# Soft-capped attention and a mixture of attention experts on one core: a bank for each warm-up product, batch 6's exponentials in loose halves, second-stage scores first, new due offsets

## The chip, the cores and the metric

The kernel runs on one NeuronCore of a Trainium2 chip. Its time is the device time of one execution in microseconds (us); before the change the median of 3 runs is 305.93 us (305.67 to 306.42).

## The reference

There are two stages. The first is attention with a soft cap, over 8 batches, 12 heads, 448 positions and 64 values a head:

```python
scores = scale * np.matmul(q, k.transpose(0, 1, 3, 2))
scores = cap * np.tanh(scores / cap)            # cap = 30
attn = np.exp(scores - scores.max(-1)); attn /= attn.sum(-1) + 1e-9
x = heads_side_by_side(np.matmul(attn, v))      # [8, 448, 768]
```

The second is a mixture of 4 attention experts, of which each position uses the best 2. Each expert is one causal head of 64:

```python
logits = x @ w_gate                             # top 2 of 4, softmax over the two: w
q, k, v = x @ wq[e], x @ wk[e], x @ wv[e]
a = causal_softmax(scale * q @ k.T)
out += w[e] * (a @ v @ wo[e])                   # only where e is among the two
```

The whole output is 8 x 448 x 768 in float32. Tiles in the kernel are float16, sums are float32.

## The kernel before, in words

**First stage.** The 12 heads of a batch are 6 pairs; over 8 batches these are pairs 0 to 47, called `p`. For each pair the queries and keys are loaded, cast, and transposed; TensorE forms the transposed scores (keys on the partitions, L956 to L972) in PSUM tiles X and Y, of three banks each (two for Y in the last part); ScalarE takes tanh from X or Y into the tile `yp` (L1018), and then exp of all of the pair in place (L1030). No maximum is subtracted, as the cap bounds the scores. TensorE multiplies with the values and a column of ones (L1044, L1051, L1091, L1098), VectorE divides (`rca`, `xk`), and the result is transposed to `xT` by TensorE or by a DMA. From pair 2 to pair 39 two pairs go together. In batch 7 the pairs 42 to 47 take only 320 of the 448 queries, and two further units 48 and 49 take the last 128 queries of all six pairs.

**Second stage.** When a batch's six pairs are done, its values, gate logits (L1196), keys and queries (L1204) come from `xT`. The gate is worked out on POOL, and becomes masks `mB` that blank the queries of experts not chosen; the masks are transposed (`mT`), and multiplied with the queries (`qm`). `b_score` (L1394) forms the scores of one half (`s` = 0 or 1, the first or the second choice) in 18 products over two banks (`H1` and `H0`, L1386), and one exp of 1024 columns writes them into `pB` (L1415). POOL blanks what is not causal, `b_pv` multiplies with the values (L1465), VectorE divides and weighs (`oB`, L1480), `b_ot` adds the halves (`oS`) and transposes them (`oT`), and `b_wo` multiplies with `wo` (L1527), copies to `ob` and stores. In units of pairs, batch 6's two halves stand at 46 and 48. Batch 7 is done apart, in `last` and `last2` (L1614, L1769), with its own exps into `pB` (L1691) and `p2` (L1815), its own `oB`-like sums in `normed` (L1552) and its last stores at L1602 and L1608.

**What sets the order.** The program builds a graph of all operations and a planner (`Graph.solve`) lays them out once, one list for each engine. ScalarE's tanh and exp are a fixed chain (`fixed=True`): their order is given, and their times in the plan give all other operations a due time, backwards along the graph. Of the operations that could start at once, an engine takes the one whose due time is earliest. `RANKS` adds offsets in hundredths of a us to the due times of single operations, by their number in the graph, from a given time of the plan on. An operation marked `first` (L1987) may be taken ahead of another one that was chosen, if its due time is near. PSUM has eight banks: A0 and A1, the third A2 (which is closed until `third` at pair 39 and then comes from Y), and those of X and Y. A `Group` holds a bank from its first operation to its last; `AUX` allows the A banks, `ANY` those of X and Y too, when their tile is not in use. On each engine instructions run in the order of the list, and an instruction that waits holds up what is behind it.

**Warm-up.** Products of a tile of zeros (`warm`) keep TensorE busy at the start: 6 of 512 columns and 35 of 128 (L1853), which have no due time but for the six:

```python
    gw = Group(AUX)
    for i in range(NWARM + NFILL):
        n = 512 if i < NWARM else 128
        pe(n, lambda n=n: nc.tensor.matmul(
            bank(gw)[:, 0:n], warm[:, 0:128], warm[:, 0:n], start=True, stop=True), ["warm"],
```

Of the kernel before, what the change touches and what calls it, by code (L numbers as in the profile page):

```python
# [25 lines left out]
    (7.5, {  # L26
        65: 646, 108: 767, 186: -94,
    }),
    (21.5, {
        191: -129, 322: 14,  # L30
    }),
    (35.5, {
        357: 88, 368: 348, 466: 221, 468: -411,
    }),
    (63.5, {
        432: 516, 554: 343, 616: 258,
    }),
    (77.5, {
        636: 695, 646: -603, 703: -641, 709: -990, 791: -13,
    }),  # L40
    (91.5, {
        810: 50, 820: 125, 873: -73, 877: -38, 880: -476,
    }),
    (105.5, {
        695: -612, 697: 532, 820: -377, 822: 211, 912: -369, 929: 381, 933: 464, 939: 1598, 949:
        515, 1026: -513, 1029: 895, 1036: 150, 1055: -784,
    }),
    (119.5, {
        976: 122, 983: 380, 990: 288, 1096: 302, 1097: 304, 1108: -37, 1109: -244, 1111: 407,
        1117: 1079, 1196: 125, 1200: 248,  # L50
    }),
    (133.5, {
        990: -504, 1009: -179, 1018: 602, 1145: -627, 1204: 594, 1205: 864, 1235: 444, 1262:
        966, 1378: -79,
    }),
    (147.5, {
        1018: -435, 1355: -175, 1359: -105, 1397: 756, 1421: -173, 1425: 295, 1431: -335, 1433:
        -92, 1437: 872, 1441: 173, 1443: 362,
    }),
    (161.5, {  # L60
        1330: 578, 1331: 361, 1344: 359, 1519: -107, 1805: -241, 1807: 149,
    }),
    (175.5, {
        1451: -385, 1456: -1234, 1463: 792, 1466: 578, 1468: 493, 1469: 793, 1579: 170, 1585:
        188, 1589: -354, 1594: 120, 1671: -161, 1674: -217, 1676: 517, 1680: 202, 1722: -164,
        1723: 589,
    }),
    (189.5, {
        1753: 139, 1760: 416, 1762: 562, 1837: 67, 1839: 107, 1843: 115,
    }),  # L70
    (203.5, {
        1777: 61, 1780: -527, 1782: -302, 1785: -404, 1839: -41, 1842: 96, 1843: -53, 1908: 233,
        1990: 117, 1993: 67, 1997: 19,
    }),
    (217.5, {
        2061: -122,
    }),
    (231.5, {
        2158: 275,
    }),  # L80
    (214.5, {
        1962: 381, 1993: 51, 1997: 83, 2086: -336, 2118: 159, 2137: -314, 2150: 1017, 2164: 31,
        2203: -393,
    }),
    (234.5, {
        2086: -835, 2161: 510, 2175: 657, 2178: 474, 2321: 577, 2324: -805, 2325: 1282, 2348:
        254, 2433: 776,
    }),
    (254.5, {
        2509: 2924, 2534: 784, 2546: 1060, 2592: -43, 2607: -322, 2609: 1259, 2615: 497, 2618:  # L90
        766, 2621: 193, 2649: 665, 2697: 184, 2707: 616, 2708: 1147, 2719: 640, 2738: 163,
    }),
# [4 lines left out]
    }),  # L97
    (239.5, {
        2155: 215, 2262: 380, 2315: 184, 2467: -521, 2499: 159, 2524: 1446, 2525: 657, 2564:
        -320, 2583: 594, 2592: 251, 2599: 529, 2600: -250, 2607: 619, 2620: 146, 2644: 1040,  # L100
        2653: 535, 2707: 430, 2738: 432,
# [4 lines left out]
SAIL = 1.1  # L106
SHIP = 1.25
# [4 lines left out]
NWARM = 6  # L112
# [15 lines left out]
XDUE = (4.354, 8.0)  # L128
# [265 lines left out]
def kernel(  # L394
# [44 lines left out]
    def sb(name, shape, dt=f16):  # L439
        return pool.tile(shape, dt, name=name)  # L440
# [100 lines left out]
    def turned(n, dst, src, r, w, name, due=None):  # L541
# [55 lines left out]
        "p (e c t) -> p e c t", e=E, c=4)  # L597
    oTL = [sb(f"oTL{i}", [128, 2, 128]) for i in range(3)]
# [412 lines left out]
    alone = {0, 1, *exps}  # L1011
# [343 lines left out]
    def b_mask(b, s):  # L1355
# [9 lines left out]
        if b < MD:  # L1365
            for r in range(2):
# [8 lines left out]
                pe(0, mm, [("mB", s), "ident"], [("mt", b, s, r)], g, occ=0.22, name=f"mT{b}")  # L1375
# [18 lines left out]
    def b_score(b, s):  # L1394
        x = b % 2
        z = "X" if b >= LB - 2 else flip()
        for part, bk in ((H1, z + "1"), (H0, z + "0")):
            for i, (o, c, q0, n) in enumerate(part):
                def mm(o=o, c=c, q0=q0, n=n):
                    ps = whole(z)[:, o // 512, :]  # L1400
# [9 lines left out]
                lead = i == 0 and part is H1  # L1410
                pe(0, mm, [("kB", x, r) for r in range(2)] + [("qm", qi(x, s), r) for r in range(2)]
                   + ([] if lead else [("z", z)]), [("s", bk)] + ([("z", z)] if lead else []), occ=2 * c_pe(n), name=f"sB{b}_{s}", takes=ZB[z] if lead else ())
        pi = 2 * (b % 2) + s
        pb = pB[pi]
        act(c_act(1024), lambda: nc.scalar.activation(  # L1415
            pb[:, 64:], TILE[z][:, 0:2, :].rearrange("p a c -> p (a c)"), AF.Exp, scale=isc),
            [("s", z + "0"), ("s", z + "1")], [("pB", pi)], fixed=True, name=f"eB{b}_{s}",
            frees=ZB[z])
        b_score.last = fixed_last()
# [35 lines left out]
    def b_pv(b, s):  # L1455
        x = b % 2
        pi = 2 * (b % 2) + s
        for n in range(4):
            g = Brief(ANY, 1.6)
            cs = cols(n)  # L1460
            for i in range(0, len(cs), 2):
                def mm(g=g, i=i, cs=cs):
                    for t in range(i, min(i + 2, len(cs))):
# [3 lines left out]
                            vB[x][:, c, :, :], start=(t == 0), stop=(t == len(cs) - 1),  # L1467
                        )

                pe(0, mm, [("pB", pi), ("pB", pi, 0), ("pB", pi, 1), (b, f"mw{s}")] + [("vB", x, c) for c, _ in cs],  # L1470
                   [("pvB", b, s, n)], g,
                   occ=0.11 * len(cs[i : i + 2]), name=f"pvB{b}_{s}")
            k_ = (2 * s + n) % 4
# [559 lines left out]
```

## Time and profile before

| what | value |
|---|---|
| median of 3 runs | 305.93 us (305.67 to 306.42) |
| profiled execution, own time | 304.88 us |
| its span, first to last instruction | 303.1 us |
| ScalarE busy | 288.8 us (95%) |
| TensorE busy | 281.1 us (93%) |
| VectorE busy | 212.4 us (70%) |
| POOL busy | 189.5 us (63%) |
| data moved by DMA | 53.12 MB, mean 175 GB/s |

The profile is one execution. Its times run from the first instruction. PE is TensorE's products, PEld its weight loads, DVE is VectorE, ACT is ScalarE, POOL is GpSimd, SP is SyncE. A row of the list of waits reads: engine, tile and line that waited, who released it, and then us in total, times, and the longest. A row of the instructions in order of time reads: start in us, duration in us, engine, line, operation, what it writes and reads, and in brackets the time that the engine stood still before it and what ended that. Rows that hold several instructions (x2 and more) give the stretch that they cover. A row of the table by stretches reads: the stretch, its length, busy time and number of instructions of PE, PEld, DVE, ACT and POOL, the granted TensorE clock, the busy share of the DMA engines, and GB/s.

### The profile page before, as it was taken

What the parts mean: (1) busy time and instruction counts of PE and PEld (TensorE: products, weight loads), DVE (VectorE), ACT (ScalarE), POOL (GpSimd) and SP (SyncE); (2) the same over time, 40 slices, a digit from 0 to 9 for tenths busy, and PEclk for the clock granted to TensorE, in tenths of its full rate; (3) what the DMA queues carried; (4) which work ended last, traced back from release to release, by engine and by line L of the source; (5) the groups of instructions that cost most, each with busy time, mean ns of one, the idle gap of its engine ahead of it and who ended that gap; (6) DMA issues with size and microseconds to landing.
All of it is one profiled execution on the core that took longest, in us unless ns stands there. A gap on an engine that the chain in (4) does not pass through costs nothing.

```text
span 303.1 us, 8923 instructions
## 1 busy us (share of the span) xinstructions
PE 281.1 (93%) x3464; PEld 191.8 (63%) x3464; DVE 212.4 (70%) x628; ACT 288.8 (95%) x208; POOL 189.5 (63%) x535
## 2 busy tenths in 40 slices
PE   8696979899999999999999999998999999999993
PEld 4353636557765668666776767656675766666761
DVE  2354527557766689588778688588777997687973
ACT  4999999999999999999999999999999999998991
POOL 6883523589955985894679952784479503831490
PEclk9999788999999999999999999999999999999999
DMA  6899989999989288786989666073407382534446
GB/s 174 213 240 195 238 202 271 223 241 260 257 229 229 63 264 224 171 212 141 297 212 193 174 180 226 23 193 118 132 7 106 81 230 33 100 61 160 73 158 208
DMA packets 86874, 53.12 MB, mean 175 GB/s; under 512 B 47536, under 2 KB 83120, under 8 KB 86832
## 3 DMA queue, kind: packets, MB, share of 16 engines
q1 hardware_dynamic: 86448, 52.13, 69.0%
q8 instruction: 27, 0.44, 0.6%
q10 hardware_dynamic: 384, 0.43, 0.4%
q14 instruction: 15, 0.12, 0.2%
HBM read 36.19 MB, written 11.01 MB: 156 GB/s over the span
## 4 chain that ended last, share of the span: by engine, by line
ACT 47%; PE 38%; DVE 9%; issue 2%; DMA 2%; SPq 0%; DVEq 0%; ACTq 0%
ACT yp L1018 23%; ACT yp L1030 22%; PE A L1051 4%; PE Y L963 3%; PE A L1527 3%; PE X L963 3%; PE A L1196 3%; PE A L1204 3%; PE A L1044 2%; ACT pP L1415 2%; DMA qf<-in_q_dram 2%; PE X L972 1%; DVE oB L1480 1%; DVE ob L530 1%; PE X L1405 1%
## 5 line engine op out<-in xcount | busy, mean ns | idle before, releaser
L1030 ACT ACTIVATE yp<-yp 128x6272 f16<-128x6272 f16 (+5 forms) x32 | 133.9, 4187 | 0.0
L1018 ACT ACTIVATE yp<-Y 128x1344 f16<-128x1344 f32 (+3 forms) x70 | 79.9, 1141 | 2.5 <-PE Y L963 2.4
L1018 ACT ACTIVATE yp<-X 128x1344 f16<-128x1344 f32 (+3 forms) x61 | 76.5, 1254 | 0.8 <-PE X L963 0.2
L1051 PE MATMUL A<-v,yp 128*128 128x65 f16 x936 | 48.3, 196 | 0.0
L1051 PEld LDWEIGHTS <-yp 128*128 128x128 f16 x1008 | 45.4, 99 | 3.0 <-issue 1.2
L1044 PE MATMUL A<-vtz,yp 128*128 128x130 f16 x156 | 35.3, 226 | 4.8 <-ACT yp L1030 3.7
L835 POOL CAST v<-vf 128x384 f16<-128x384 f32 x48 | 24.1, 509 | 23.1 <-PE A L1051 12.8
L1073 DVE RECIPROCAL rca<-A 128x4 f32<-128x4 f32 x78 | 14.2, 182 | 34.1 <-PE A L1051 33.7
L1076 DVE TENSOR_TENSOR xk<-A,rca 128x256 f16<-128x256 f32 x78 | 33.0, 424 | 2.4
L799 POOL CAST q<-qf 112x512 f16<-112x512 f32 x44 | 26.7, 618 | 11.5 <-PE A L849 9.0
L1044 PEld LDWEIGHTS <-yp 128*128 128x128 f16 x168 | 16.5, 98 | 20.1 <-issue 13.6
L784 POOL CAST k<-kf 128x384 f16<-128x384 f32 x33 | 16.9, 521 | 15.9 <-DMA kf<-in_k_dram 8.7
L908 DVE COPY qk<-A 128x960 f16<-128x960 f16 x32 | 20.6, 651 | 8.8 <-PE A L849 8.5
L1425 POOL TENSOR_SCALAR_AFFINE_SELECT pP<-pP 128x384 f16<-128x384 f16 x14 | 7.4, 527 | 22.1 <-ACT pP L1415 22.1
L963 PE MATMUL X<-qk 64*128 64x448 f16 x102 | 18.6, 358 | 2.0 <-ACT yp L1018 1.3
L963 PE MATMUL Y<-qk 64*128 64x448 f16 x102 | 19.2, 367 | 1.4 <-ACT yp L1030 0.5
L849 PE MATMUL A<-ident,q 112*128 112x112 f16 x192 | 19.4, 214 | 0.1
L1490 POOL TENSOR_TENSOR oS<-oB,oB 128x512 f16<-128x512 f16 x14 | 16.1, 1154 | 4.4 <-issue 3.8
L1196 PEld LDWEIGHTS <-xT 128*128 128x128 f16 x168 | 15.7, 97 | 3.9 <-issue 1.2
L963 PEld LDWEIGHTS <-qk 64*128 64x128 f16 x204 | 10.3, 93 | 11.4 <-issue 3.7
L1196 PE MATMUL A<-wvg,xT 128*128 128x260 f16 x126 | 17.4, 274 | 0.1
L530 DVE COPY ob<-A 128x384 f32<-128x384 f32 (+1 forms) x30 | 16.2, 552 | 1.8 <-PE A L1527 1.3
(319 smaller groups left out, 677.5 us busy)
## 6 DMA issues: line engine op xcount, KB each, us to landing
qf<-in_q_dram SPq DMA_DIRECT2D x23, 448.0 KB, 6.4
kf<-in_k_dram SPq DMA_DIRECT2D x23, 384.0 KB, 5.2
vf<-in_v_dram SPq DMA_DIRECT2D x23, 384.0 KB, 5.4
out_dram<-ob SPq DMA_DIRECT2D x21, 384.0 KB, 3.2
ktf<-in_k_dram SPq DMA_DIRECT2D x46, 32.0 KB, 4.9
vtf<-in_v_dram SPq DMA_DIRECT2D x46, 32.0 KB, 4.5
out_dram<-ob SPq DMA_DIRECT2D x6, 192.0 KB, 3.2
ob<-in_moe_wv_dram SPq DMA_DIRECT2D x2, 384.0 KB, 5.3
```

The costliest lines, as they stand in the source:

```text
L530: (nc.scalar.copy if o.eng == "ACT" else nc.vector.tensor_copy)(dst(), src())
L799: e(q16[i], qf[s][:, h].rearrange("p h (c d) -> p c h d", c=QC))
L835: nc.gpsimd.tensor_copy(v16[u][:, :, :, 0:Dh], vf[s][:, h].rearrange("p h (c d) -> p h c d", c=KC))
L849: nc.tensor.transpose(ps[:, 0:S].rearrange("m (g c t) -> m c g t", c=QC, t=16)[:, c], q16[i][:, c, :, :].rearrange("p h d -> p (h d)"), id ...
L908: lambda: nc.vector.tensor_copy(qk[t], bank16(g)[:, 0 : S + 512]),
L963: nc.tensor.matmul(dst[:, bank0 + g - gs[0], 0:n], keysT(p)[r, 128 * (c + 1) : 128 * (c + 2)], qk[p % NQK][r, 0:n], start=True, stop=True)
L1018: ACTS[what, p] = act(c_act(n * k), lambda: nc.scalar.activation(y[:, lo : lo + k, 0:n], TILE[z][:, 0:k, 0:n], AF.Tanh, scale=isc / capf), ...
L1030: act(c_act(n * (b - a), False), lambda a=h + a, b=h + b: nc.scalar.activation(y[:, a:b, 0:n], y[:, a:b, 0:n], AF.Exp, scale=capf), ks, ks ...
L1044: nc.tensor.matmul(ps[:, n, :, :], y[:, o : o + 128], vtz[u], start=(n == 0), stop=False, skip_group_check=True,)
L1051: nc.tensor.matmul(ps[:, n, h, :], y[:, o : o + 128], v16[u][:, h, c, :], start=False, stop=(c == 2), skip_group_check=True,)
L1076: dve(c_dve(128 * m), lambda g=g, i=i, rc=rc, m=m: nc.vector.tensor_tensor(xk[p % NXK][:, 2 * i : 2 * i + m, :, :], view(g)[:, 0:m, :, 0:D ...
L1196: nc.tensor.matmul(bank(g)[:, 0 : E * Dh + E], xT[x][:, j, WIN[n] : WIN[n] + 128], wvg[:, j, :], start=(j == j1), stop=(j == jn),)
```

## The change

- The warm-up products: the six of 512 columns share one bank, which is free again behind the sixth, and each of the 35 small ones takes a bank for itself alone.
- Batch 6's two halves (`LOOSE`): the scores of each go to two single banks of any kind in place of tile X, and each bank has its own exp of 512 columns, which is no part of ScalarE's fixed chain. Units 46 and 48 are no longer kept apart from their neighbours (`alone`), so that their products are filled in one go with the next unit's.
- Batch 7's exps write to `pL`, in the upper half of one tanh tile that is free by then, and no longer to `pB`; its weighted sums go to `oBL`, in the tile of the first mask, and no longer to `oB`. So neither waits for batch 6. An empty operation (`pLfree`) stands behind the last reader of that half.
- The score products of the second stage (`sB`) are marked `first`.
- Two orders are added in the graph: the masks' transposes wait for the batch's queries `qB` (and come before their use in `qm`), and a value product waits for the last reader of the reciprocal that its group will write.
- `XDUE` of the second entry goes from 8.0 to 9.5: the due time of the `xT` transposes of units of two pairs.
- `RANKS` is another table: 17 times with 179 offsets, where there were 21 with 178.

```diff
 RANKS = (
-    (7.5, {
-        65: 646, 108: 767, 186: -94,
+    (-0.5, {
+        57: 299, 58: 555, 65: 250, 102: 331, 110: 231, 133: 142, 140: 456, 174: -71, 185: -241,
+        187: -135, 188: -70, 191: -135,
     }),
...
+LOOSE = (0, 1)
...
-XDUE = (4.354, 8.0)
+XDUE = (4.354, 9.5)
...
+    PF = ("yp", (PB + 5) // 2 % 2)
+    free3 = yf[PF[1]][:, 7 * S : 7 * S + 4 * 704].rearrange("p (i c) -> p i c", c=704)
+    pL = [free3[:, 2 * i : 2 * i + 2] for i in range(2)]
+    oBL = mB[0].rearrange("p a b c d -> p (a b c d)").rearrange("p (n e d) -> p n e d", n=4, e=E)
...
-    alone = {0, 1, *exps}
+    alone = {0, 1, *(p for p, (b, s) in exps.items() if b < LB - 1 or s not in LOOSE)}
...
-                pe(0, mm, [("mB", s), "ident"], [("mt", b, s, r)], g, occ=0.22, name=f"mT{b}")
+                pe(0, mm, [("mB", s), "ident", ("qB", x, r)], [("mt", b, s, r), ("qm", qi(x, s), r)], g,
+                   occ=0.22, name=f"mT{b}")
...
+        pi = 2 * (b % 2) + s
+        pb = pB[pi]
+        free = b == LB - 1 and s in LOOSE
         z = "X" if b >= LB - 2 else flip()
-        for part, bk in ((H1, z + "1"), (H0, z + "0")):
+        for part, h in ((H1, 1), (H0, 0)):
+            g = Group(ANY, 1.5) if free else None
             for i, (o, c, q0, n) in enumerate(part):
-                def mm(o=o, c=c, q0=q0, n=n):
-                    ps = whole(z)[:, o // 512, :]
+                def mm(o=o, c=c, q0=q0, n=n, g=g):
+                    ps = bank(g) if g else whole(z)[:, o // 512, :]
...
+            if free:
+                act(c_act(512), lambda g=g, h=h: nc.scalar.activation(
+                    pb[:, 64 + 512 * h : 576 + 512 * h], bank(g), AF.Exp, scale=isc),
+                    [("sf", b, s, h)], [("pB", pi)], g, name=f"eF{b}_{s}")
+        if not free:
+            act(c_act(1024), lambda: nc.scalar.activation(
+                pb[:, 64:], TILE[z][:, 0:2, :].rearrange("p a c -> p (a c)"), AF.Exp, scale=isc),
+                [("s", z + "0"), ("s", z + "1")], [("pB", pi)], fixed=True, name=f"eB{b}_{s}",
+                frees=ZB[z])
...
-                   [("pvB", b, s, n)], g,
+                pe(0, mm, [("pB", pi), (b, f"mw{s}")] + [("vB", x, c) for c, _ in cs],
+                   [("pvB", b, s, n)] + [("rcb", (2 * s + n) % 4)] * (i == 0), g,
...
-            oB[0][:, n], view(g)[:, :, 0:Dh], sl.broadcast_to((128, E, Dh)), ALU.mult),
-            [key, ("slL", n)], [("oB", 0, n)], g, name="oBL")
+            oBL[:, n], view(g)[:, :, 0:Dh], sl.broadcast_to((128, E, Dh)), ALU.mult),
+            [key, ("slL", n)], [("oBL", n), ("mB", 0)], g, name="oBL")
...
-                    pB[pi][:, o : o + W1], bank(g2[e])[:, 0:W1], AF.Exp, scale=isc),
-                    [k0 if e == 0 else ("sL", r, part, 2)],
-                    [("pB", pi, part)] + ([("pB", pi)] if part == 0 else []), g2[e],
+                    pL[r][:, e, o : o + W1], bank(g2[e])[:, 0:W1], AF.Exp, scale=isc),
+                    ["pLfree", k0 if e == 0 else ("sL", r, part, 2)],
+                    [("pL", pi, part)], g2[e],
...
+        pe(0, lambda: None, [], ["pLfree"] + [PF + (7 + w,) for w in range(7)], occ=0.0,
+           name="op")
...
-    gw = Group(AUX)
+    gw = None
     for i in range(NWARM + NFILL):
         n = 512 if i < NWARM else 128
-        pe(n, lambda n=n: nc.tensor.matmul(
+        gw = gw if 0 < i < NWARM else Group(AUX)
+        pe(n, lambda n=n, gw=gw: nc.tensor.matmul(
...
-        o.first = o.name[:2] in ("sX", "sY", "sT", "tr", "qk", "k1", "q1", "ge", "kt")
+        o.first = o.name[:2] in ("sX", "sY", "sT", "sB", "tr", "qk", "k1", "q1", "ge", "kt")
```

More of the change, by code (lines that the diff above doesn't have):

```diff
@@ L47 @@
+    (39.5, {
+        353: 7, 363: 458,
+    }),
+    (55.5, {
+        363: 202, 397: 312, 423: 134, 517: -1175, 554: -388, 573: -91,
+    }),
+    (71.5, {
+        616: 16, 646: -377, 706: 26, 760: 369, 840: 414,
+    }),
+    (87.5, {
+        787: 218, 788: 44, 810: -103, 882: 769,
+    }),
+    (103.5, {
+        695: 942, 943: 646, 1029: 190, 1074: 913,
     }),
     (119.5, {
-        976: 122, 983: 380, 990: 288, 1096: 302, 1097: 304, 1108: -37, 1109: -244, 1111: 407,
-        1117: 1079, 1196: 125, 1200: 248,
-    }),
@@ L102 @@
+    (244.5, {
+        2315: 136, 2499: 43, 2502: -20, 2503: 624, 2517: 165, 2520: -72, 2523: 373, 2527: -330,
+        2528: 303, 2537: 294, 2606: 983, 2622: -414, 2643: -132, 2650: -2605, 2689: -794, 2713:
+        -1257, 2732: -1268, 2745: 1153,
     }),
@@ L1408, in mm @@
                                 )
-                lead = i == 0 and part is H1
+                lead = i == 0 and h == 1 and not free
                 pe(0, mm, [("kB", x, r) for r in range(2)] + [("qm", qi(x, s), r) for r in range(2)]
[L1412 to L1419, printed above, removed]
+                   + ([] if lead or free else [("z", z)]),
+                   [("sf", b, s, h)] if free else [("s", f"{z}{h}")] + ([("z", z)] if lead else []), g,
+                   occ=2 * c_pe(n), name=f"sB{b}_{s}", takes=ZB[z] if lead else ())
+            if free:
[7 more added lines that the diff above has]
+                frees=ZB[z])
         causal(pb, pi, "")
@@ L1572, in mt @@
                     bank16(gt)[:, 128 * r : 128 * (r + 1)],
-                    oB[0][:, n, 2 * r : 2 * r + 2, :].rearrange("p e d -> p (e d)"), ident)
-        pe(0, mt, [("oB", 0, n), "ident"], [("otL", n)], gt, occ=0.11, name="oTL")
+                    oBL[:, n, 2 * r : 2 * r + 2, :].rearrange("p e d -> p (e d)"), ident)
+        pe(0, mt, [("oBL", n), "ident"], [("otL", n)], gt, occ=0.11, name="oTL")
         lo = 64 if n == 2 else 0
@@ L1701, in below @@
                         pattern=[[0, 2], [1, 128]], channel_multiplier=-1)
-                gp(0.38, below, [], [("pB", pi, part) for pi in (2 * r, 2 * r + 1)], name="diagL")
+                gp(0.38, below, [], [("pL", pi, part) for pi in (2 * r, 2 * r + 1)], name="diagL")
+        pe(0, lambda: None, [], ["pLfree"] + [PF + (7 + w,) for w in range(7)], occ=0.0,
+           name="op")
         for part in range(2):
```

73 lines of the change are left out of this document (21 added, 52 removed), and 11 rows, old and new, of the table RANKS.

## The prediction

> **What bounds the kernel now.** I read the page first (busy times, slices), then ScalarE's list of waits, then its instructions in order of time at the head and at the end, then TensorE's and VectorE's beside them, and the table by stretches.
>
> ```profile
> span 303.1 us, 8923 instructions
> PE 281.1 (93%) x3464; PEld 191.8 (63%) x3464; DVE 212.4 (70%) x628; ACT 288.8 (95%) x208; POOL 189.5 (63%) x535
>
> ACT yp L1018 <- PE Y L963: 2.4, 2, 1.8
> ACT pP L1415 <- PE X L1405: 1.7, 2, 1.1
> ```
>
> ScalarE (ACT) is busy for 288.8 of 303.1 us, so 14.3 us is all that it stands still, and only two kinds of waits inside its row of tanh and exp are worth anything: score products that come late (2.4 us, of which 1.8 is the head), and the second stage's scores that come late (1.7 us in two places). The rest is the head before the first tanh and the tail behind the last exp. The table by stretches (PE, PEld, DVE, ACT, POOL busy) says how the end differs from the middle:
>
> ```profile
> 20.00:60.00 40.00, 33.57 (x369) 20.52 (x366) 21.17 (x64) 39.13 (x24) 18.10 (x45) 0.91 1.04 232
> 275.00:280.00 5.00, 4.97 (x73) 3.36 (x72) 3.87 (x9) 3.88 (x4) 0.76 (x2) 1.00 0.21 59
> 280.00:285.00 5.00, 5.00 (x65) 3.92 (x62) 4.65 (x18) 5.00 (x5) 1.34 (x2) 1.00 0.29 84
> 285.00:290.00 5.00, 5.00 (x72) 3.82 (x71) 3.70 (x12) 4.41 (x11) 4.36 (x14) 1.00 0.42 56
> 295.00:303.10 8.10, 2.96 (x24) 1.41 (x22) 3.24 (x10) 1.78 (x5) 0.52 (x2) 1.00 0.61 205
> ```
>
> From 275 to 290 us TensorE has no gap at all, and ScalarE loses 1.12 us at 275 to 280. Behind 295 us nobody is full: that is the latency of the last tile's chain. So ScalarE's row sets when the last exp ends, and the last tile's chain, with TensorE full at its start, adds its length to that.
>
> ```profile
> 274.09 2.11 ACT L1030 ACTIVATE yp<-yp 128x2240 f16<-128x2240 f16 x1
> 277.29 1.02 ACT L1415 ACTIVATE pP<-X 128x1024 f16<-128x1024 f32 x1 [1.08 <-PE X L1405]
> 278.21 0.80 ACT L1018 ACTIVATE yp<-Y 128x768 f16<-128x768 f32 x1
> 283.79 2.54 ACT L1030 ACTIVATE yp<-yp 128x1920 f16<-128x1920 f16 x2
> 293.58 0.63 ACT L1815 ACTIVATE yp<-X0s 128x512 f16<-128x512 f32 x1
> 294.06 0.64 ACT L1815 ACTIVATE yp<-X2s 128x512 f16<-128x512 f32 x1
> 298.96 0.34 SPq L1602 DMA_DIRECT2D out_dram<-kf  x1
> ```
>
> The fixed row ends at 283.79 + 2.54 = 286.33 us; the last store is issued at 298.96, and the span ends 16.77 us behind the last exp. The profiled execution took 304.88 us, 1.78 more than its span; the median of the runs is 305.93, 1.05 above it. I sum against 304.88 and add 1.05 at the end.
>
> **Part 1: the head (a bank for each warm-up product).** Before, all 41 warm-up products share one PSUM bank, which is held until the last of them; as A2 is shut at the start, A1 alone is left for the first transposes.
>
> ```profile
> 4.32 0.41 ACT L818 CAST q<-qf 112x256 f16<-112x256 f32 x1 [0.32 <-DMA qf<-in_q_dram]
> 4.63 0.47 ACT L866 COPY qk<-A 128x384 f16<-128x384 f16 x1
> 5.16 0.53 PE L849 MATMUL A<-ident,q 112*128 112x112 f16 x4
> 6.39 0.22 PE L914 MATMUL A<-ident,ktz 128*128 128x128 f16 x1
> 6.94 0.55 DVE L799 CAST q<-qf 112x512 f16<-112x512 f32 x1 [0.74 <-DMA qf<-in_q_dram]
> 7.41 0.21 DVE L917 COPY qk<-A 128x128 f16<-128x128 f16 x1
> 6.95 0.92 ACT L1018 ACTIVATE yp<-Y 128x896 f16<-128x896 f32 x1 [1.84 <-PE Y L963]
> 8.07 1.29 ACT L1018 ACTIVATE yp<-X 128x1344 f16<-128x1344 f32 x1 [0.20 <-PE X L972]
> 15.15 0.36 PE L963 MATMUL Y<-qk 64*128 64x448 f16 x2 [0.50 <-ACT yp L1030]
> 15.80 0.93 ACT L1018 ACTIVATE yp<-Y 128x896 f16<-128x896 f32 x1
> ```
>
> The q halves are cast by 4.73, but the q transposes (L849) start at 5.16, just behind the copy (4.63 + 0.47 = 5.10) that empties A1. With a second bank they could start at about 4.80: the first tanh moves from 6.95 to 6.59. The second tanh gains only if the tail copy L917 no longer stands behind the cast L799, which waits for its load: the transpose L914 is done at 6.61, a copy then, the tail product (0.36, as the one at 15.15) and the tanh give about 7.4 in place of 8.07. That is the upper bound, 0.67 us. The lower is none: pair 2's first products come at 15.15, ready at 15.51, only 0.29 before ScalarE takes them at 15.80, and a head that is earlier by more has to find them earlier too. I take the middle, -0.35. What is late next is that product.
>
> **Part 2: the second stage's scores first.** Now the planner may put other products between them:
>
> ```profile
> 188.30 0.45 PE L1405 MATMUL X<-qm,kB 128*128 128x256 f16 x4
> 188.59 1.50 PE L1196 MATMUL A<-wvg,xT 128*128 128x260 f16 x12
> 190.81 1.02 ACT L1415 ACTIVATE pP<-X 128x1024 f16<-128x1024 f32 x1 [0.59 <-PE X L1405]
> 33.17 1.29 ACT L1018 ACTIVATE yp<-Y 128x1344 f16<-128x1344 f32 x1 [0.52 <-PE Y L963]
> ```
>
> Twelve value products (1.50) stand between the first four and the other score products, and ScalarE waits 0.59. Marked as first, the scores are chosen ahead of work that is due later. I take -0.5; the ends are -0.59 and +0.5 (a wait like the one at 33.17, if the scores push the first stage's products back). The twelve products are late next, behind them the gate's steps on POOL, for which ScalarE does not wait.
>
> **Part 3: batch 6's exponentials as four loose halves.** Two fixed instructions leave the row. Each keeps ScalarE for 278.21 - 277.29 = 0.92 us, and the second makes it wait for 1.08: -2.92 for the end of the row. Four halves of 512 come in, each worth 294.06 - 293.58 = 0.48. In the row they cost 1.92 and the net is -1.0; behind the row, where ScalarE idles, the net is -2.92. Their due time comes from stores that are due late, so they give way to fixed work, but they will fill a gap where there is one. Between the ends I put two inside and two behind: -2.92 + 0.96 = -1.96. Splitting by itself costs 2 x 0.48 - 0.92 = 0.04 each.
>
> The Trainium skill speaks against the split here ("ScalarE: Activation LUTs", section "What ACT_TABLE_LOAD costs"): an instruction costs 186 ns beside 0.833 ns an element, and back-to-back ones overlap by about 93 ns. By that, an estimate, two halves cost 0.09 us more than the whole, 0.19 for the batch where the rows give 0.08; the sum would be 0.1 us higher. The trace does not bear out so large a price.
>
> **Part 4: the end.** The halves' products go to single banks of any kind in place of tile X, which was held for scores and exp; X's next tanh can be filled earlier. Against this, batch 6's tail work moves back to where TensorE is full.
>
> ```profile
> 265.25 1.06 PE L1405 MATMUL X<-qm,kB 128*128 128x256 f16 x18
> 279.95 0.76 PE L1465 MATMUL A<-vB,pP 128*128 128x260 f16 x5
> 280.55 0.50 PE L1465 MATMUL X0s<-vB,pP 128*128 128x260 f16 x3
> 281.54 0.40 PE L1465 MATMUL A<-vB,pP 128*128 128x260 f16 x2
> 287.08 0.44 ACT L1691 ACTIVATE pP<-X2s 128x320 f16<-128x320 f32 x1
> 105.62 0.63 DVE qB L1191
> ```
>
> One head half's scores are 18 products (1.06), its value products here 0.76 + 0.50 + 0.40 = 1.66. Moved behind 286 they push the last tile's chain by up to 1.66; but as many products of the last batch then move ahead, and from 295 on TensorE works 2.96 of 8.1 us, so much of it fits there. The bounds are -0.5 (X free earlier) and +1.7; I take +0.5. The new buffers (pL in the unused upper half of a tanh buffer, oBL in the mask's tile) let the last batch's exps start before batch 6 is read; now they start at 287.08, over 5 us behind batch 6's value products at 281.54, so nothing is gained by this alone: it only pays for part 3.
>
> Priced at nothing: mask transposes wait for qB (0.63 us on VectorE, four batches; ScalarE never waits there; if one came to the path, 0.63), value products wait for the reciprocal's reader four groups back, XDUE 9.5 delays xT copies by up to 1.5 us, which the batch's end needs much later. The new table of offsets re-orders everything; the one before has 178 offsets, this one 179, so I give it no term, only width.
>
> Sum: -0.35 - 0.5 - 1.96 + 0.5 = -2.31; 304.88 - 2.31 = 302.57; with 1.05, **303.6 us**. Its own range, with half of each term's width, is 302.2 to 305.0.
>
> **The rivals.**
>
> *Banks (slower).* Between 262 and 286 us only three A banks serve transposes, value products and output products. A half holds one from its first product until its exp is done; if ScalarE is in a 2.11 us exp (the row at 274.09), the bank is out for that much longer, and TensorE, in order and without gaps, may stand at a product that has no bank. Behind it stand the next scores, for which ScalarE waits. One half so caught costs up to 2.1 us; two give 303.6 + 4.2 = 307.8. It decides from 3.3 us lost (306.9) on. For it: TensorE 4.97 to 5.00 of 5. Against: tile X, two banks long, is freed.
>
> *The tail eats it (same).* If the last tile's chain, not ScalarE's row, is what TensorE delays, the 1.96 is given back: 305.6. For it: no TensorE gap from 275 to 290 us; against: the 1.12 us that ScalarE stood still there.
>
> *All of it (faster).* Four halves behind the row, the head's bound, no price at the end: 304.88 - 0.67 - 0.59 - 2.92 + 1.05 = 301.8.
>
> *The clock.* The granted clock is 0.91 between 20 and 60 us, and a product takes longer there; ScalarE's 0.52 at 33.17 lies in such a spell (slice digit 7). A third spell gives 303.6 + 0.5 = 304.1, more if it meets several fills. The Trainium skill says why it may move ("TensorE: Matmul & The Clock Gate", section "What's actually happening"): the array runs at half clock until it was busy for a free-running window of some 3.4 us, so changed warm-up products can shift it. The low digits 7, 8, 8 fit that; where the next would fall no row here shows.
>
> **How the numbers follow.** Chances: forecast 0.42, all of it 0.13, the clock 0.07 (these three are faster), the tail 0.13, banks 0.25. No change is told from one by about 0.3% (0.92 us), so faster means below 305.0, slower above 306.9: 0.62, 0.13, 0.25. The range goes to 301.2 below (some 0.04 left out) and to 307.8 above (half of the banks' case left out).
>
> **What would show it.** Part 1: first tanh before 6.7 us, the second before 7.8, and pair 2's first tanh before 15.6. Part 2: no wait of ScalarE behind L1405's products between 100 and 260 us. Part 3: no 1024-wide exp behind 262 us, four of 512 in their place, and the last fixed exp's end at 283 to 285 us. Part 4: from that end to the end of the span 16.5 to 17.5 us. Wrong it would be if ScalarE shows new waits for L956 or L963 behind 262 us (banks), if the tail behind the last exp grows by 2 us or more, or if the new order loses time in the middle, where I left it alone.

## The result, and the profile after

The changed kernel takes 303.13 us (median; 302.53 to 303.42), the one before 305.80 us (305.16 to 306.42) beside it: a ratio of 0.991 with the interval 0.9884 to 0.9936. That is 0.9% faster, and 0.5 us from the forecast of 303.6. The profiled execution took 303.0 us and its span is 301.2, so 1.9 us less than before by both.

The page and ScalarE's list of waits of the kernel after:

```profile
span 301.2 us, 8936 instructions
PE 282.4 (94%) x3464; PEld 191.4 (64%) x3464; DVE 212.5 (71%) x628; ACT 288.5 (96%) x210; POOL 189.8 (63%) x535
```

```profile
ACT yp L1011 <- PE Y L956: 2.0, 2, 1.5
...
ACT yp L1011 <- PE X L965: 0.6, 2, 0.4
```

L1011 is the tanh, L956 and L965 the first stage's score products, L1403 those of the second stage, L1418 the whole exps, L1414 the new halves. ScalarE is as busy as before (288.5 for 288.8); what went is standing still. No wait for `pP` is left.

To see where, I follow the same ScalarE instruction through both traces and subtract its starts. ScalarE's instructions in order of time, after:

```profile
6.61 0.92 ACT L1011 ACTIVATE yp<-Y 128x896 f16<-128x896 f32 x1 [1.49 <-PE Y L956]
7.46 1.29 ACT L1011 ACTIVATE yp<-X 128x1344 f16<-128x1344 f32 x1
10.10 1.29 ACT L1011 ACTIVATE yp<-X 128x1344 f16<-128x1344 f32 x1 [0.43 <-PE X L965]
15.59 0.93 ACT L1011 ACTIVATE yp<-Y 128x896 f16<-128x896 f32 x1
25.09 0.92 ACT L1011 ACTIVATE yp<-X 128x896 f16<-128x896 f32 x1 [0.52 <-PE A L1044]
46.71 1.00 ACT L1011 ACTIVATE yp<-X 128x896 f16<-128x896 f32 x1
184.15 5.74 ACT L1023 ACTIVATE yp<-yp 128x6272 f16<-128x6272 f16 x1
189.47 1.33 ACT L1418 ACTIVATE pP<-X 128x1024 f16<-128x1024 f32 x1
265.68 0.79 ACT L1011 ACTIVATE yp<-Y 128x640 f16<-128x640 f32 x1
271.94 1.23 ACT L1414 ACTIVATE pP<-A 128x512 f16<-128x512 f32 x2
272.93 2.20 ACT L1023 ACTIVATE yp<-yp 128x2240 f16<-128x2240 f16 x1
277.28 1.24 ACT L1414 ACTIVATE pP<-A 128x512 f16<-128x512 f32 x2
278.24 2.62 ACT L1023 ACTIVATE yp<-yp 128x2688 f16<-128x2688 f16 x1
281.26 2.72 ACT L1023 ACTIVATE yp<-yp 128x1920 f16<-128x1920 f16 x2
```

And the rows of the kernel before that answer to them and are not shown yet:

```profile
46.89 0.92 ACT L1018 ACTIVATE yp<-X 128x896 f16<-128x896 f32 x1 [0.25 <-PE X L963]
266.63 1.11 ACT L1415 ACTIVATE pP<-X 128x1024 f16<-128x1024 f32 x1
267.81 0.70 ACT L1018 ACTIVATE yp<-Y 128x640 f16<-128x640 f32 x1
```

| place | before | after | lead | change of it |
|---|---|---|---|---|
| first tanh | 6.95 | 6.61 | -0.34 | -0.34 |
| pair 2's first tanh | 15.80 | 15.59 | -0.21 | +0.13 |
| last tanh of the next two pairs | 23.99 | 25.09 | +1.10 | +1.31 |
| last tanh of the pairs two steps on | 46.89 | 46.71 | -0.18 | -1.28 |
| the exp ahead of one of the second stage's | 184.52 | 184.15 | -0.37 | -0.19 |
| that second-stage exp | 190.81 | 189.47 | -1.34 | -0.97 |
| start of batch 6's last part | 266.63 | 265.68 | -0.95 | +0.39 |
| end of the row, 281.26 + 2.72 | 286.33 | 283.98 | -2.35 | -1.40 |
| end of the span | 303.1 | 301.2 | -1.9 | +0.45 |

So the gain comes from two places, a second-stage exp that no longer waits and batch 6's exps; the head's gain is small, and a loss of 1.31 us at 16 to 25 us is paid back by 47 us. The table by stretches, after (columns as before), shows the end and the place of that loss:

```profile
16.40:19.80 3.40, 1.67 (x16) 1.05 (x16) 0.66 (x1) 3.40 (x3) 3.29 (x18) 1.00 0.96 229
19.80:23.20 3.40, 2.74 (x19) 1.19 (x19) 0.74 (x2) 2.97 (x3) 2.21 (x10) 0.50 1.03 247
23.20:26.60 3.40, 3.40 (x48) 2.93 (x48) 1.59 (x6) 2.80 (x3) 2.20 (x6) 0.50 0.69 149
275.00:280.00 5.00, 5.00 (x76) 4.00 (x74) 4.21 (x15) 5.00 (x7) 0.76 (x2) 1.00 0.00 0
280.00:285.00 5.00, 4.90 (x73) 3.92 (x72) 4.78 (x19) 4.57 (x6) 3.05 (x5) 1.00 0.14 30
```

At 275 to 280 us ScalarE is now busy for 5.00 of 5 us (3.88 before). From 19.8 to 26.6 us the granted clock is 0.50 and ScalarE loses 1.03 us (0.43 and 0.60). Before had two such spells, each half as long, later on:

```profile
30.30:33.70 3.40, 3.36 (x44) 2.54 (x45) 1.57 (x5) 2.88 (x3) 1.57 (x4) 0.53 0.97 232
43.70:47.10 3.40, 3.40 (x40) 2.10 (x38) 1.64 (x6) 3.15 (x4) 0.44 (x2) 0.51 0.95 339
```

The waits at 33.17 and 46.89 lie in them, and after has neither.

### The profile page after: what moved, and what is told of

It is laid out like the page before. It is cut to its first block, busy times and chain, and to the rows that moved or that the text cites. A ratio compares the mean times of both kernels' runs of the same rounds, so it can differ in the third digit from the quotient of the medians.

```text
span 301.2 us, 8936 instructions
## 1 busy us (share of the span) xinstructions
PE 282.4 (94%) x3464; PEld 191.4 (64%) x3464; DVE 212.5 (71%) x628; ACT 288.5 (96%) x210; POOL 189.8 (63%) x535
## 4 chain that ended last, share of the span: by engine, by line
ACT 65%; PE 23%; POOL 4%; issue 3%; DVE 2%; DMA 1%; ACTq 0%; POOLq 0%; DVEq 0%
ACT yp L1023 31%; ACT yp L1011 31%; ACT pP L1418 3%; PE A L1044 2%; PE A L1529 2%; PE Y L956 2%; PE X L956 2%; DMA ktf<-in_k_dram 1%; PE A L1189 1%; PE A L1037 1%; PE A L1871 1%; PE X L1403 1%; PE A L842 1%; PE X L965 1%; PE A L1595 1%
## 5 line engine op out<-in xcount | busy, mean ns | idle before, releaser
L1023 ACT ACTIVATE yp<-yp 128x6272 f16<-128x6272 f16 (+5 forms) x32 | 136.3, 4269 | 0.0
L1011 ACT ACTIVATE yp<-Y 128x1344 f16<-128x1344 f32 (+3 forms) x70 | 85.1, 1216 | 2.0 <-PE Y L956 2.0
L1011 ACT ACTIVATE yp<-X 128x1344 f16<-128x1344 f32 (+3 forms) x61 | 81.6, 1339 | 1.1 <-PE X L965 0.6
L1044 PE MATMUL A<-v,yp 128*128 128x65 f16 x924 | 46.6, 195 | 0.0
L1069 DVE TENSOR_TENSOR xk<-A,rca 128x256 f16<-128x256 f32 x77 | 32.3, 422 | 2.1
L1037 PEld LDWEIGHTS <-yp 128*128 128x128 f16 x168 | 16.5, 98 | 16.0 <-issue 12.9
L956 PE MATMUL X<-qk 64*128 64x448 f16 x102 | 19.4, 371 | 4.2 <-ACT yp L1011 3.4
L519 DVE COPY ob<-A 128x384 f32<-128x384 f32 (+1 forms) x37 | 19.8, 553 | 2.2 <-PE A L1529 1.6
L956 PE MATMUL Y<-qk 64*128 64x448 f16 x102 | 19.2, 368 | 2.1 <-ACT yp L1011 0.8
L956 PEld LDWEIGHTS <-qk 64*128 64x128 f16 x204 | 11.1, 94 | 14.5 <-issue 7.8
L842 PEld LDWEIGHTS <-q 112*128 112x128 f16 x192 | 14.1, 100 | 5.9 <-issue 1.8
L1529 PE MATMUL A<-wo,oT 128*128 128x384 f16 x78 | 17.8, 326 | 0.1
```

Of the source, the lines that this page charges most:

```text
L519: (nc.scalar.copy if o.eng == "ACT" else nc.vector.tensor_copy)(dst(), src())
L842: nc.tensor.transpose(ps[:, 0:S].rearrange("m (g c t) -> m c g t", c=QC, t=16)[:, c], q16[i][:, c, :, :].rearrange("p h d -> p (h d)"), id ...
L956: nc.tensor.matmul(dst[:, bank0 + g - gs[0], 0:n], keysT(p)[r, 128 * (c + 1) : 128 * (c + 2)], qk[p % NQK][r, 0:n], start=True, stop=True)
L1011: ACTS[what, p] = act(c_act(n * k), lambda: nc.scalar.activation(y[:, lo : lo + k, 0:n], TILE[z][:, 0:k, 0:n], AF.Tanh, scale=isc / capf), ...
L1023: act(c_act(n * (b - a), False), lambda a=h + a, b=h + b: nc.scalar.activation(y[:, a:b, 0:n], y[:, a:b, 0:n], AF.Exp, scale=capf), ks, ks ...
L1037: nc.tensor.matmul(ps[:, n, :, :], y[:, o : o + 128], vtz[u], start=(n == 0), stop=False, skip_group_check=True,)
```

## The experiments

The theory is the prediction's: each edit is worth its own term, and the new offsets are only width. The first rival is that an offset table is fitted to one set of rules, so that the parts cannot be told apart under it; others are named where they are tested. Ratios are to the kernel before on the same chip. Where operations are added or left out, the offsets were kept with their operations and not with their numbers.

**One bank for the warm-up products again.**

```diff
-        gw = gw if 0 < i < NWARM else Group(AUX)
+        gw = gw or Group(AUX)
```

> The changed kernel with all 41 warm-up products in one bank again, as before; all else, the offsets too, as changed. Theory A (the gain is made in four places by the four edits, and the head's 0.2 us is the only thing that the banks give): the first tanh goes back from 6.61 to about 6.95 us, the keep-warm products of 512 columns (first at 31.4 in the changed kernel, at 11.8 before) come early again, the half-clock spell of 20 to 27 us goes or shrinks, and with it ScalarE's two waits of 0.52; in sum between 0.2 slower and 1.0 us faster than the changed kernel's 303.1. Theory B (the order from the offsets makes the gain, whatever the edit): the plan no longer fits its offsets and the time is 303.5 to 304.5 with new waits all over.

Measured: 320.72 us, ratio 1.0517 (1.0476 to 1.0557). That is far above what either theory expected. The head shows the mechanism, in a row of TensorE and one of ScalarE:

```profile
5.69 0.36 PE L842 MATMUL A<-ident,q 112*128 112x112 f16 x4 [0.76 <-ACT qk L859]
```

```profile
4.86 0.40 ACT L811 CAST q<-qf 112x256 f16<-112x256 f32 x1 [0.92 <-DMA qf<-in_q_dram]
```

The q transposes wait for the copy that empties the bank, as the prediction had it, and the first tanh starts at 7.16 us, for 6.61 after. Not all of that is the bank's: the load of the queries landed later in this profile, so that their cast starts at 4.86 us and not at 4.32 as in after. And most of the 5% is elsewhere: the planner's order differs from about 4 us on, the later offsets meet another state, and waits appear up to the last batch (one of 5.0 us at L1819). What an edit is worth cannot be read from this kernel.

**The keep-warm products not chained to the warm-up.** After, the 36 large keep-warm products of the middle stand behind the small ones, which wait for banks until 31 us; before they ran from 11.8 us. Is that the cause of the half-clock spell?

```diff
-                   ["warm", ("tick", p, what)], ["warmps"], g, name="fill")
+                   ["warm", ("tick", p, what)], ["keepps"], g, name="fill")
```

> The changed kernel with one key altered: the keep-warm products of 512 columns are no longer ordered behind the 35 small warm-up products. Theory A: the half-clock spell at 20 to 27 us in the changed kernel comes from keep-warm products that are held back behind the small ones, each of which now waits for a bank; freed, they run from about 11 us, the spell goes or is halved, the two waits of 0.52 at 23.3 and 25.1 us shrink, and the time is 302.0 to 302.8. Rival: the spell comes from TensorE's work itself at 17 to 20 us, the keep-warm products find no bank or no gap, and the time stays at 303.1 within 0.4.

Measured: 303.37 us, 0.9942 (0.9918 to 0.9966), the same as after within the intervals. The spell is there all the same; stretch and TensorE row of this kernel:

```profile
20.40:26.80 6.40, 6.34 (x69) 4.31 (x69) 2.52 (x8) 5.36 (x6) 3.06 (x10) 0.50 0.93 178
```

```profile
20.46 0.90 PE L956 MATMUL X<-qk 64*128 64x448 f16 x3 [2.35 <-ACT yp L1011]
```

The keep-warm products now begin at 11.1 us, and TensorE still stands at 18 to 20.46 us with a score product that has no tile. That theory fell. The transposes of the following pairs are half done at that time; that they hold both A banks, so that nothing else can run, is argued and was not tried.

**Batch 6's exps whole and in the chain again, all else as after.**

```diff
-LOOSE = (0, 1)
+LOOSE = ()
```

> The changed kernel with batch 6's two exps whole, fixed and in tile X again (LOOSE empty); offsets kept, each for the same operation. Theory A: ScalarE's row gets back 2 x 0.92 in place of about 1.95 and a wait of up to 1.1 at each of the two; the last fixed exp ends 1.0 to 1.6 us later than 283.98, the stretch behind it stays near 17, and the time is 304.0 to 304.8. Theory B: 303.1 within 0.4.

Measured: 311.22 us, 1.0196 (1.016 to 1.0231). The row of ScalarE that tells it:

```profile
274.06 1.02 ACT L1423 ACTIVATE pP<-X 128x1024 f16<-128x1024 f32 x1 [8.81 <-PE X L1407]
```

Up to 256 us the order on TensorE is that of after. Then one wait of 8.81 us is all of the loss (2.86% more than after, 8.7 us), more than either theory had. The exp's fixed place is at 265 us, but under the new offsets batch 6's queries come at 269.19 (12 products, 2.45 us) and its scores at 272.89 (L1407). After can do that, because a loose exp comes when its scores do (271.94). So the offsets have used the freedom, and the edit and the offsets cannot be priced apart here.

**Second-stage scores not first, all else as after.**

```diff
-        o.first = o.name[:2] in ("sX", "sY", "sT", "sB", "tr", "qk", "k1", "q1", "ge", "kt")
+        o.first = o.name[:2] in ("sX", "sY", "sT", "tr", "qk", "k1", "q1", "ge", "kt")
```

> The changed kernel with the second stage's scores not marked first; offsets kept. Theory A: ScalarE's wait for batch scores in front of the 1024-wide exp near 190 us comes back (0.6 us, 0.97 with what stood before it), and the time is 303.7 to 304.2. Rival: the new offsets already put the scores early, and it is 303.1 within 0.4.

Measured: 311.19 us, 1.0213 (1.0178 to 1.0248). TensorE's order is the same up to about 70 us; from there on ScalarE waits for the scores in one batch after the other:

```profile
ACT pP L1418 <- PE Y L1403: 3.8, 3, 1.6
ACT pP L1418 <- PE X L1403: 2.3, 2, 2.0
```

6.1 us of waits where after has none. At the predicted place the list names POOL:

```profile
193.54 1.02 ACT L1418 ACTIVATE pP<-X 128x1024 f16<-128x1024 f32 x1 [1.01 <-POOL g_h L1304]
```

But its scores (L1403, 18 products from 192.39 us, 1.06 long) end at 193.45, just ahead of it, so this wait may be theirs too. The kind of wait and the place are the predicted ones; the time is not (303.7 to 304.2 was expected), and the size is again edit and misfit together.

**The floor without offsets.** Undoing one edit under a table that was made for it measures the misfit too. So both kernels were run with no offsets, and each with the other's table.

```diff
+RANKS = ()
```

> The kernel before with an empty table of offsets. It is the floor from which the next run is read. The offsets are worth much: the four runs above, where an edit was undone and the offsets kept, were up to 16 us slower, so 312 to 330 us is expected.

> The changed kernel with an empty table of offsets. Theory A (the edits themselves make the gain): 2 to 8 us less than the kernel before without offsets, most of it from the scores that are marked first (waits for the batch scores fewer by 3 us or more). Theory B (only the new table makes it): within 1 us of the kernel before without offsets, or slower.

> The code before with the new offsets, each for the same operation. Theory A, in which edits and offsets were fitted to one another: well over 306, near 311 or more, with waits for the batch scores as where the scores are not marked first, and about 9 us before batch 6's first exp. Theory B: 303 to 304.5.

> The changed code with the offsets of before, each for the same operation. If the edits gain by themselves: 303 to 305. If edits and offsets only fit together: 308 to 322, with a new order from the first microseconds on.

| ratio to before (interval) | no offsets | table of before | table of after |
|---|---|---|---|
| code before | 1.0494 (1.0459 to 1.0528) | 1 | 1.054 (1.05 to 1.0579) |
| code after | 1.0333 (1.0301 to 1.0365) | 1.0384 (1.0343 to 1.0426) | 0.991 (0.9884 to 0.9936) |

One per cent is 3.06 us here. Without offsets the edits give 1.0494 - 1.0333 = 1.6%, or 4.9 us. Each table gives its own code a lot (4.9%, 15.1 us, before; 1.0333 - 0.991 = 4.2%, 12.9 us, after) and the other code nothing (1.054 and 1.0384, neither below its floor). So "the offsets re-order everything" holds, but they are no mere width around the edits: counted along the column without offsets, the 0.9% of the change are 1.6% from the edits less 0.7% by which the new table gains less than the old one did. Counted along another column the two parts have other sizes. Both crossed kernels (two executions each) came out as the theory of edits and offsets fitted together had it, except that the old code with the new table has no wait at batch 6's first exp (283.45 us); its longest, 7.8 us, ends at a tanh 3.4 us earlier. The waits of ScalarE for the second stage's scores in the kernel before, without offsets, are these:

```profile
ACT pP L1337 <- PE X L1327: 5.6, 3, 2.5
...
ACT pP L1337 <- PE Y L1327: 4.3, 1, 4.3
```

**One edit at a time undone, without offsets.** The same diffs as above, each added to the kernel after without offsets (1.0333).

> The changed kernel without offsets and with the second stage's scores not marked first; to be read against the changed kernel without offsets, 315.6 us. Theory A2 (of the 5.1 us that the edits give without offsets, the scores marked first give most): 318 to 321. Rival: the loose halves give it; 315.6 to 317.

> The changed kernel without offsets and with batch 6's exps whole and fixed in tile X; against 315.6 us. If the loose halves give what I forecast for the row (about 2 us, less 0.5 at the end): 316.5 to 318. If they give most of the 5.1 us: 319 to 321. If nothing: 315.6 within 0.5.

> The changed kernel without offsets and with all warm-up products in one bank; against 315.6 us. The banks by themselves give a head that is 0.2 to 0.6 us earlier, and hold the keep-warm products back: 315.2 to 316.2, with the first tanh near 7 us. Where the time of the run with offsets (16 us slower) came from the edit itself and not from offsets that no longer fit, it is above 320.

| left out | ratio (interval) | less 1.0333 | row ends | from there to the end |
|---|---|---|---|---|
| nothing | 1.0333 (1.0301 to 1.0365) | | 288.33 | 26.5 |
| scores first | 1.0436 (1.0382 to 1.049) | 1.0%, 3.1 us | 291.44 | 25.5 |
| loose halves | 1.034 (1.0293 to 1.0388) | 0.1%, 0.2 us | 293.14 | 20.6 |
| a bank each | 1.0391 (1.0338 to 1.0445) | 0.6%, 1.8 us | 289.27 | 26.4 |

The three add up to 1.7%, and all edits together make 1.6%; the other parts of the change were not undone alone, and this sum leaves nothing for them beyond the intervals. The intervals of "a bank each" and of the floor overlap a little, so its 1.8 us are the least sure (at most 0.6 was expected); between the two profiled spans it is 0.9 (315.7 and 314.8), where the floor's is its longest of four. Each row is one plan: by how much a plan without offsets moves when something is altered that should not matter was not tried.

Scores first: one row of waits says it, of the kernel without offsets first, then of the one that also lacks the mark.

```profile
ACT pP L1352 <- PE X L1337: 0.6, 2, 0.4
```

```profile
ACT pP L1352 <- PE X L1337: 5.5, 3, 3.1
```

Loose halves: without them the row ends 4.8 us later, with this wait in it, and yet the time is the same.

```profile
274.75 1.02 ACT L1352 ACTIVATE pP<-X 128x1024 f16<-128x1024 f32 x1 [4.37 <-PE X L1337]
```

What the row lost, the end had in hand: 20.6 us in place of 26.5 behind it. Without offsets the last batch's chain is the bound; with the halves ScalarE's row is done early and ScalarE then waits for 3.46 us for the gate's values, as this row of the kernel without offsets shows:

```profile
293.25 0.38 ACT L453 CAST vB<-A 128x256 f16<-128x256 f32 x1 [3.46 <-DVE gt L1596]
```

That is the prediction's rival "the tail eats it". It is the case without offsets, and not with them.

A bank each: the first TensorE rows of the kernel without offsets, then of the one with one shared bank.

```profile
4.68 0.55 PE L776 MATMUL A<-ident,q 112*128 112x112 f16 x4
6.12 0.56 PE L890 MATMUL Y<-qk 64*128 64x448 f16 x2
```

```profile
5.10 0.55 PE L776 MATMUL A<-ident,q 112*128 112x112 f16 x4
6.35 0.36 PE L890 MATMUL Y<-qk 64*128 64x448 f16 x2
```

The q transposes start 0.42 us earlier with a bank each, as predicted. Of that 0.23 are left at the first scores, since the transpose between waits 0.67 us for POOL's cast of keys (5.55), and that 1.39 us for their load; and the scores still take 0.56 us, at half clock, where the shared bank's kernel is at full clock (0.36), so the first tanh gains 0.03 only (6.72 for 6.75). The us by which the profiles differ comes later: about 46 us the same tanh starts at 46.48 with a shared bank and at 45.48 without, and the shared bank's kernel has waits for L890 behind slow products, such as three score products that take 0.92 us from 34.51 on (clock 0.50 from 34.0 to 35.4, where the other has 1.00). In these two profiles the bank edit's worth comes in spells of half clock and not at the head; that the edit is what moves the spells is not shown.

**Is it that the halves are loose, or that their place is later?** The exps whole and fixed, but later, at units 48 and 49 in place of 46 and 48, with the offsets of after.

```diff
-LOOSE = (0, 1)
+LOOSE = ()
...
-        XOFF if b < LB - 2 else (4, 6))}
+        XOFF if b < LB - 2 else (4, 6) if b < LB - 1 else (6, 7))}
```

> The changed kernel, offsets kept, with batch 6's exps whole and fixed in tile X, but at units 48 and 49 in place of 46 and 48. It tells being loose from being late. If the 8.8 us wait of the run with both fixed at 46 and 48 came from a place in ScalarE's row that is ahead of the batch's queries: no wait over 1 us for L1403's products, the last fixed exp ends 283.5 to 285.5, and the stretch behind it grows, since the second half comes some 4 us later than in the changed kernel: 304 to 307. If it came from tile X itself, the wait stays, and the time is over 309.

Measured: 312.86 us, 1.0219 (1.0152 to 1.0286). ScalarE's rows:

```profile
274.16 1.02 ACT L1423 ACTIVATE pP<-X 128x1024 f16<-128x1024 f32 x1 [0.51 <-PE X L1408]
279.96 1.03 ACT L1423 ACTIVATE pP<-X 128x1024 f16<-128x1024 f32 x1
```

The row ends at 281.55 + 2.56 = 284.11, within 0.13 of after, with one wait of 0.51: for the row a later place is as good as loose halves, and tile X was not the cause of the 8.81 us. The time, though, lies well above the 304 to 307 that were expected with this. But the second exp comes 2.7 us later than the loose one (279.96 for 277.28), and behind the row stand 26.9 us, against 17.2 in after; batch 6's output products (L1534, six at 304.09, two at 305.06) are the last of all. So what the loose halves seem to give under these offsets is the best place in each of two respects: late enough for the row and early enough for the end. That the whole loss against after (3.1%, 9.4 us) comes from this one delay is not shown, since the offsets of the end do not fit this kernel either.

## Why the prediction was right, point by point

**The sum.** Most of the mechanism held, but that the forecast is within 0.5 us is in part luck. Between the two profiles the terms make -1.9 us (303.0 - 304.88) and not -2.31. Against that, the 1.05 us by which the median lay above the profile of before, and which the forecast adds at the end, are only 0.13 after (303.13 - 303.0). The first miss is upwards by 0.43 and the second downwards by 0.92. Three smaller things in the prediction are off: half of the way to each term's bounds gives 302.4 to 305.4 and not 302.2 to 305.0; the last store before is issued at 299.20 us, by ScalarE's queue, and not at 298.96; and the premise of the banks rival, that only the A banks serve value products, does not agree with its own row of L1465 into `X0s` at 280.55.

**Part 1, the head.** Forecast -0.35; measured -0.34 at the first tanh, -0.61 at the second (8.07 to 7.46) and, where it counts, -0.21 at pair 2's (a wait of 0.43 at 10.10, behind products that are still slow, takes back 0.39). All three signs held (6.61, 7.46 and 15.59 against 6.7, 7.8 and 15.6), the last by 0.01 us. The way there was only half right. The transposes did start earlier, at 4.68 us for 5.16; the predicted 4.80 was the right row. What is late next was named wrongly. After shows on TensorE a transpose of keys that waits for POOL, on POOL a cast that waits for its load, and then score products at half clock:

```profile
4.68 0.56 PE L842 MATMUL A<-ident,q 112*128 112x112 f16 x4
5.79 0.29 PE L907 MATMUL A<-ident,ktz 128*128 128x128 f16 x1 [0.56 <-POOL ktz L822]
6.01 0.56 PE L956 MATMUL Y<-qk 64*128 64x448 f16 x2
```

```profile
5.44 0.29 POOL L822 CAST ktz<-ktf 128x128 f16<-128x128 f32 x1 [1.29 <-DMA ktf<-in_k_dram]
```

**The clock.** The rival's event came: a new half-clock spell at 19.8 to 26.6 us, beside which 1.3 us were lost, more than the 0.5 in its sum. Its price did not, since the two spells that before had at 30 and 44 us are gone with their waits, and by 47 us the loss is paid back. The Trainium skill ("TensorE: Matmul & The Clock Gate", section "What's actually happening") has full clock return behind at least one busy window of some 3.4 us. Before agrees, with two spells of about 3.4 us. After's spell is as long as two such windows, which does not speak against that: in the first half TensorE stood still until 20.46 us (2.74 of 3.40 busy), in the second it was busy throughout (3.40 of 3.40), and then full clock came. How busy a window must be is not shown: with the keep-warm products freed the first half had 3.14 of 3.40 us, and the spell was as long, while 3.16 of 3.40 us (30.1 to 33.5) were enough before.

**Part 2, scores first.** The sign held: no wait behind the second stage's scores from 100 to 260 us. Forecast -0.5; at that exp it was -0.97. The term was mis-sized because it counted only the idle time. In after the exp ahead of it (184.15) is followed by the next instruction 5.32 us on, though it lasts 5.74: back-to-back instructions overlap, by 0.42 here. Behind a wait the overlap is lost, so that a wait of 0.59 costs nearly 1 us. 0.39 us were given back before 266 us, and the sum at that place, -0.95, is about what parts 1 and 2 had together (-0.85).

**Part 3, loose halves.** Forecast -1.96, measured -1.40. The step that failed is "two inside and two behind": all four halves went into the row, as two pairs ahead of exps of 2240 and 2688 columns (272.93 - 271.94 = 0.99 and 278.24 - 277.28 = 0.96, so 1.95 in place of 0.96). That alone would have given -1.0, the upper end. The other term was too small as well. After has the same exp of 2240 columns without a wait ahead of the next instruction (265.68):

```profile
263.71 2.16 ACT L1023 ACTIVATE yp<-yp 128x2240 f16<-128x2240 f16 x1
```

Before, the first whole exp kept ScalarE for 267.81 - 266.63 = 1.18, the second for 0.92, and the wait for 3.20 - 1.97 = 1.23, when 277.29 - 274.09 is set against 265.68 - 263.71: 3.33 and not 2.92. 1.95 - 3.33 = -1.38 is what the lead shows. Splitting costs 0.04 to 0.07 for a whole exp of 0.92 (0.96 and 0.99 for two halves). The Trainium skill ("ScalarE: Activation LUTs", section "What ACT_TABLE_LOAD costs") would have 0.09, and the trace stays below it.

**Part 4, the end.** Forecast +0.5, measured +0.45 (17.22 us behind the row for 16.77); the promised 16.5 to 17.5 held. The way there did not: the prediction let the value products of two halves move behind 286 us and push the last tile's chain. After has all of batch 6's value products from 274.53 us on and inside the row, the last of them here:

```profile
280.73 0.39 PE L1467 MATMUL A<-vB,pP 128*128 128x260 f16 x2
```

Before, the last stood at 281.54, so they moved ahead by less than the row's end did (0.81 for 2.35), and TensorE is full beside them, with 5.00 and 4.90 of 5 us in the two stretches shown. From the end of the row to the last store's issue it is 13.62 us (297.60) for 12.87, so +0.75, and 0.30 less stand behind that. What of the +0.75 is batch 6's was not tried, and that the size came out is luck in part. The banks rival did not come: there are no waits of ScalarE from 262 to 282 us in after.

**The offsets.** "No term, only width" is the step that was right in the sum and wrong as a view. The two tables differ by 0.7%, 2.2 us, which goes the other way than the edits. The terms fitted because they were read off the waits that remained under the table of before: 1.7 us for `pP` in all. Without offsets the same kernel has 5.6 + 4.3 = 9.9 us of them, so the old table had already taken most of what "first" is for. That this is why the new table gains less is argued from these numbers, not shown.

## What to carry to other kernels

Offsets that were fitted to an order belong to the code they were fitted on: undo an edit under them and the misfit is measured (9 to 18 us here, for edits of 0 to 3), so set edits against each other without them, and judge the tuned pair by itself. To place a gain, follow the same instruction through both traces and read the lead; a wait costs its idle time and the overlap that it breaks. A looser place for work need not be worth anything by itself; look at what comes behind it, since a row that ends 5 us earlier can leave the time where it was.

## What the runs showed of the hardware that was not expected

The head moves by more than a us between kernels whose order there is the same. The kernel with the scores not first has the order of after up to 70 us, yet its rows on TensorE, POOL and ScalarE are:

```profile
5.58 0.36 PE L956 MATMUL Y<-qk 64*128 64x448 f16 x2
```

```profile
4.89 0.29 POOL L822 CAST ktz<-ktf 128x128 f16<-128x128 f32 x1 [0.75 <-DMA ktf<-in_k_dram]
```

```profile
8.84 1.29 ACT L1011 ACTIVATE yp<-X 128x1344 f16<-128x1344 f32 x1
```

Two things differ. The load of the keys lands 0.55 us earlier (the cast at 4.89 for 5.44), and full clock is there earlier: the score products take 0.36 us at 5.58, where those of after take 0.56 at 6.01 and 0.48 still at 9.29. The first tanh is 0.62 us earlier (5.99), the fourth 1.26 (8.84 for 10.10), and at 45.44 for 46.71 it still is. So the head of one profile carries about 1 us of the load's and the clock's moments, three times the head's term, and a difference there needs the products' durations and the loads beside it. The Trainium skill ("TensorE: Matmul & The Clock Gate", section "What's actually happening") warns that this moment varies from run to run, and the trace agrees; it holds the ramp for less than 1% of a span, and 1.27 of 301.2 us is 0.4%, but that is more than the 0.3% that can be told apart here.

Half clock also came with short gaps: after's spell begins in one of 1.70 us (18.76 to 20.46), behind 3.4 us with 1.67 us of products in them. Yet the amount of work in such a stretch does not decide it alone. The kernel with the scores not first has as little in this one, and the clock is 1.00 in it and in the 3.4 us behind it:

```profile
38.70:42.10 3.40, 1.66 (x20) 1.03 (x20) 1.49 (x3) 3.40 (x3) 1.27 (x4) 1.00 0.96 275
```

What sets the phase, and what is counted, is open.
